# Moving the first FC1 block to just behind head 7, and transposing heads 8 and 9 by DMA between the weight loads, in a fused attention and FFN kernel

## The chip, the cores and the metric

The kernel runs on one core of one Trainium2 chip. The metric is the device time of one execution in microseconds (us), taken on the slowest core, of which there is one here. Several executions are timed and their median is quoted, with the range in brackets. Every run used below was in the fast state, with a granted TensorE clock of 0.998 to 1.0, except where a lower one is named.

PE is the tensor engine (matmuls), ACT the scalar engine, DVE the vector engine, POOL is GpSimd, and SP the engine that issues most DMAs here. "L228" in a profile line is line 228 of that kernel's source.

## The reference, cut to what matters

The attention has B·H = 32 heads of 768 tokens and 64 dimensions. Each q and each k row is assigned to its nearest of 16 centroids, and a query sees only those keys that have its own cluster. The output goes through a feed-forward network with weights 512x2048 and 2048x512.

```python
q_assign = argmax(einsum('bhsd,hcd->bhsc', q_n, c_n))      # k_assign alike
mask     = q_assign[:, :, :, None] == k_assign[:, :, None, :]
scores   = where(mask, scale * q @ k.T, -1e9)
attn     = exp(scores - max) / (sum + 1e-9)
x        = (attn @ v) as (3072 tokens, 512)
h        = x @ w_in                                         # FC1
out      = (gelu(h) @ w_out)                                # FC2, exact gelu
```

## The kernel before

Everything is written by hand into one list of timed events; the "times" only decide the program order of each engine, and each engine then works through its own instructions in that order. For each head, POOL splits q and k (fp32) into a high and a low fp16 half. The 128-token tiles are transposed to `T` (channels on the partitions). PE computes the assignment scores (`asn`), DVE turns them into one-hot rows `oh`, and those are transposed too and written into 16 additional rows of `T`, so that the score matmul adds the mask by itself. ACT exponentiates, PE multiplies by v (the "AV" matmuls), DVE normalises.

There are two ways to transpose. Heads below `PT` use PE with a copy out of PSUM by DVE; the later ones use the DMA transpose, issued from SP:

```python
def tr_pe(i, w, copy=None, pool=None):                      # 6 PE transposes, one copy
    ...
    for j in range(N):
        nc.tensor.transpose(t_ps[:, j*128:(j+1)*128], st[:, w, j, :], ident)
    (copy or nc.vector.tensor_copy)(Ts[i][:, w, :], t_ps)

def tr(i):                                                  # one DMA for q and k
    nc.sync.dma_start_transpose(out=Ts[i]..., in_=st...)

def asn(i, which, halves=True):                             # 6 short matmuls for q or k
    if which == 0:
        asns[i] = ps_a.tile([128, 512], FP32, tag="asn", name="asn_ps")   # ps_a has ONE buffer
    ...
def onehot(i, halves=True): ...                             # three DVE instructions, frees asn_ps
def ohtr(i): ...                                            # one DMA transpose for two heads
def aug(i):                                                 # four DVE copies ohT -> rows 64..79 of T
    ...
PT = 10
FC1 = {(9, 3): 0, (18, 0): 1, (26, 0): 2}                   # FC1 of batch 0 in head 9, slot 3
for n in range(1, 8):
    at(T[n] + 0.5, load_w, n)                               # one weight chunk per head, from POOL
for h in range(4, NH):
    ...                                                     # split, v cast, load of head h + 4
    if h >= PT:
        at(max(T[pair] - {10: 25.0, 12: 25.0, 14: 35.0}.get(pair, 29.0) + ..., sp_t + 3.5), tr, h)
for h in range(PT, NH):
    ...                                                     # asn, onehot, ohtr and aug, ahead of need
```

Each head has six slots: a score matmul pair, a few FC2 matmuls as filler once FC1 has run (`FILL`), AV of the head before. FC1 itself is one dense block of some 21 us per batch.

The softmax here doesn't subtract the row's maximum and nothing guards it: scores larger than these inputs give would overflow.

Of the kernel before, what the change touches and what calls it, by code (L numbers as in the profile page):

```python
# [20 lines left out]
def kernel(  # L21
# [64 lines left out]
    load(1)  # L86
    nc.sync.dma_start(out=v_raw, in_=v[0, 0].rearrange("(p n) d -> p n d", p=128))
    load(2)
    load(3)
# [57 lines left out]
    def tr_pe(i, w, copy=None, pool=None):  # L147
        if i not in Ts:
            Ts[i] = t_pool.tile([128, 2, S], FP16, tag="T", name="T")
        st = sts[i]  # L150
        pl, tag = pool or (ps_o, "op")
        t_ps = pl.tile([128, S], FP16, tag=tag, name="tr_ps")
        for j in range(N):
            nc.tensor.transpose(t_ps[:, j * 128:(j + 1) * 128], st[:, w, j, :], ident)  # L154
        (copy or nc.vector.tensor_copy)(Ts[i][:, w, :], t_ps)  # L155
# [23 lines left out]
    tr_pe(0, 0, copy=nc.scalar.copy, pool=(ps_sc, "sc"))  # L179
    warm(1, 256)  # L180
    nc.vector.tensor_scalar_add(cent_norm, cent_norm, 1e-6)
    nc.vector.reciprocal(cent_rnorm, cent_norm)
    nc.vector.tensor_tensor(cent_hl[:, 0], cent_sb.unsqueeze(1).to_broadcast([H * C, 2, D]),
                            cent_rnorm.unsqueeze(2).to_broadcast([H * C, 2, D]), op=ALU.mult)
# [13 lines left out]
    def tr_halves(i, w):  # L198
        for e, (pl, tag, copy) in enumerate(((ps_sc, "sc", nc.scalar.copy),
                                             (ps_o, "op", nc.vector.tensor_copy))):  # L200
            t_ps = pl.tile([128, S], FP16, tag=tag, name="tr_ps")
            for j in range(N // 2):
                nc.tensor.transpose(t_ps[:, j * 128:(j + 1) * 128],
                                    sts[i][:, w, e * (N // 2) + j, :], ident)
            copy(Ts[i][:, w, e * QB:(e + 1) * QB], t_ps[:, 0:QB])
# [12 lines left out]
    def asn(i, which, halves=True):  # L218
# [6 lines left out]
        for j in range(N):  # L225
# [4 lines left out]
            else:  # L230
                for e in range(2):
                    nc.tensor.matmul(a_ps[:, j, which, 0], t[:, js], c_all[:, e, chs],
                                     start=(e == 0), stop=(e == 1))

# [34 lines left out]
    def one_pe(i):  # L269
        oh = ohs[(i // 2) % NOH]  # L270
        e = i % 2
        t_ps = ps_o.tile([128, S], FP16, tag="op", name="oh_ps")
        for j in range(N):
            nc.tensor.transpose(t_ps[:, j * 128:(j + 1) * 128],
                                oh[:, j].rearrange("p a b c -> p (a b c)"), ident)
        nc.vector.tensor_scalar(Ts[i][D:D + C, 1, :], t_ps[64 * e + 32:64 * e + 32 + C, :],  # L276
                                -1.0, None, op0=ALU.add)
        nc.vector.tensor_scalar(Ts[i][D:D + C, 0, :], t_ps[64 * e:64 * e + C, :],  # L278
                                float(VAL), None, op0=ALU.mult)
# [69 lines left out]
    def fin(i, pe=False):  # L349
        b, h = divmod(i, H)  # L350
        m = h // 2
        if m == 0:
            xts[b] = x_pool.tile([128, NM, S], FP16, tag="xt", name="xt")
        xt, x_tok = xts[b][:, m, :], xtoks.pop(i)
        if pe:
            pl, tag = (ps_a, "asn") if i == 6 else (ps_o, "op")
            t_ps = pl.tile([128, S], FP16, tag=tag, name="fin_ps")
            for j in range(N):
                nc.tensor.transpose(t_ps[:, j * 128:(j + 1) * 128],  # L359
                                    x_tok[:, j].rearrange("p a d -> p (a d)"), ident)  # L360
            nc.vector.tensor_copy(xt, t_ps)
        else:
            nc.sync.dma_start_transpose(
                out=xt.rearrange("c (n p) -> c n p", p=128),
                in_=x_tok.rearrange("p n a d -> p (n a d)"))
# [3 lines left out]
    early = []  # L369

    def fc1_early():
        for t in range(2):
            early.append(ps_o.tile([128, 512], FP32, tag="op", name="hp_early"))
        for m in range(NM - 1):
            for t in range(2):
                nc.tensor.matmul(early[t][:, 0:QB], w_in_sb[:, m, 0:128],
                                 xts[0][:, m, t * QB:(t + 1) * QB],
                                 start=(m == 0), stop=False)
                yield

    def fc1(b, f):
        if f == 0:
            gs[b] = []
        if b == 0 and f == 0:
            g = g_pool.tile([128, S], FP16, tag=f"g{f}", name=f"g{f}")
            for t in range(2):
                ts = slice(t * QB, (t + 1) * QB)
                nc.tensor.matmul(early[t][:, 0:QB], w_in_sb[:, NM - 1, 0:128],
                                 xts[0][:, NM - 1, ts], start=False, stop=True)
            gs[b].append(g)  # L390
        else:
            hp = ps_sc.tile([128, 2, 512], FP32, tag="sc", name="hp")
            for m in range(NM):
                for t in range(2):
                    nc.tensor.matmul(hp[:, t, 0:QB],  # L395
                                     w_in_sb[:, m, f * 128:(f + 1) * 128],
                                     xts[b][:, m, t * QB:(t + 1) * QB],
                                     start=(m == 0), stop=(m == NM - 1))
            g = g_pool.tile([128, S], FP16, tag=f"g{f}", name=f"g{f}")
            nc.scalar.activation(g.rearrange("p (t q) -> p t q", t=2),  # L400
                                 hp[:, :, 0:QB], ACT_FN.Gelu, bias=0.0, scale=1.0)
            gs[b].append(g)
            if b == 0 and f == 1:
                for t in range(2):
                    nc.scalar.activation(gs[0][0][:, t * QB:(t + 1) * QB], early[t][:, 0:QB],
                                         ACT_FN.Gelu, bias=0.0, scale=1.0)
# [22 lines left out]

    def load_w(n):  # L430
        nc.gpsimd.dma_start(out=w_chunks[n][0], in_=w_chunks[n][1])


    warm(1)
    cent_tr()
    tr_halves(0, 1)
    nc.scalar.copy(sts[1][:, 1, :, 0:D], k1_raw)
    nc.gpsimd.tensor_sub(sts[1][:, 1, :, D:2 * D], k1_raw, sts[1][:, 1, :, 0:D])
    warm(1)
    asn(0, 0, halves=False)  # L440
    asn(0, 1, halves=False)
    onehot(0, halves=False)
# [25 lines left out]
    def slot(i, c):  # L468
# [5 lines left out]
        if i >= 10:  # L474
# [5 lines left out]
    def start_early():  # L480
        filler[0] = fc1_early()

    def start_fc2(b):
# [3 lines left out]
    PT = 10  # L487
    FC1 = {(9, 3): 0, (18, 0): 1, (26, 0): 2}
# [3 lines left out]
        (0, 0): ((1, 'trk'),),  # L492
        (0, 1): ((1, 'asq'),),
        (0, 2): ((1, 'ask'), (1, 'oneh'),),
        (0, 3): ((2, 'trq'),),
        (0, 4): ((1, 'onep'),),
        (0, 5): ((2, 'trk'), (2, 'asq'),),
        (1, 0): ((3, 'trq'),),
        (1, 1): ((2, 'ask'), (2, 'oneh'), (3, 'trk'),),
        (1, 2): ((0, 'av0'), (0, 'av1'),),  # L500
        (1, 3): ((0, 'av2'), (2, 'onep'),),
        (1, 4): ((3, 'asq'), (3, 'ask'), (0, 'av3'), (3, 'oneh'),),
        (1, 5): ((0, 'av4'), (0, 'av5'), (0, 'norm'),),
        (2, 0): ((4, 'trq'),),
        (2, 1): ((3, 'onep'),),
        (2, 2): ((1, 'av0'), (1, 'av1'),),
        (2, 3): ((4, 'trk'), (4, 'asq'),),
        (2, 4): ((1, 'av2'), (1, 'av3'), (4, 'ask'),),
        (2, 5): ((1, 'av4'), (1, 'av5'),),
        (3, 0): ((4, 'oneh'), (1, 'norm'), (5, 'trq'),),  # L510
        (3, 1): ((4, 'onep'),),
        (3, 2): ((2, 'av0'), (2, 'av1'), (2, 'av2'),),
        (3, 3): ((5, 'trk'), (5, 'asq'),),
        (3, 4): ((0, 'fin'), (2, 'av3'), (5, 'ask'),),
        (3, 5): ((2, 'av4'), (2, 'av5'),),
        (4, 0): ((5, 'oneh'), (2, 'norm'), (6, 'trq'),),
        (4, 1): ((5, 'onep'),),
        (4, 2): ((3, 'av0'), (3, 'av1'),),
        (4, 3): ((6, 'trk'), (6, 'asq'),),
        (4, 4): ((3, 'av2'), (3, 'av3'), (6, 'ask'),),  # L520
        (4, 5): ((3, 'av4'), (3, 'av5'),),
        (5, 0): ((6, 'oneh'), (3, 'norm'), (7, 'trq'),),
        (5, 1): ((6, 'onep'),),
        (5, 2): ((4, 'av0'), (4, 'av1'), (7, 'asq'),),
        (5, 3): ((7, 'trk'), (4, 'av2'),),
        (5, 4): ((2, 'fin'), (7, 'ask'),),
        (5, 5): ((4, 'av3'), (4, 'av4'), (4, 'av5'),),
        (6, 0): ((7, 'oneh'), (4, 'norm'), (8, 'trq'),),
        (6, 1): ((7, 'onep'),),
        (6, 2): ((5, 'av0'), (5, 'av1'),),  # L530
        (6, 3): ((8, 'trk'), (5, 'av2'),),
        (6, 4): ((5, 'av3'), (8, 'asq'), (8, 'ask'),),
        (6, 5): ((8, 'oneh'), (5, 'av4'), (5, 'av5'), (5, 'norm'),),
        (7, 0): ((9, 'trq'),),
        (7, 1): ((8, 'onep'),),
        (7, 2): ((6, 'av0'), (6, 'av1'),),
        (7, 3): ((9, 'trk'), (9, 'asq'),),
        (7, 4): ((6, 'av2'), (6, 'av3'), (9, 'ask'),),
        (7, 5): ((6, 'av4'), (9, 'oneh'), (6, 'av5'),),
        (8, 0): ((6, 'norm'), (4, 'fin'),),  # L540
        (8, 1): ((9, 'onep'),),
        (8, 2): ((7, 'av0'), (7, 'av1'),),
        (8, 3): ((7, 'av2'),),
        (8, 4): ((7, 'av3'), (7, 'av4'),),
        (8, 5): ((7, 'av5'),),
        (9, 0): ((7, 'norm'),),
        (9, 1): ((6, 'fin'),),
        (9, 2): ((8, 'av0'),),
        (9, 3): ((8, 'av1'),),
        (9, 4): ((8, 'av2'), (8, 'av3'),),  # L550
        (9, 5): ((8, 'av4'), (8, 'av5'),),
        (10, 0): ((8, 'norm'),),
# [7 lines left out]
    for i in range(NH + 1):  # L560
        for c in range(N):
            if (i, c) in FC1:
                b = FC1[i, c]
                at(t, fill, 1000)
                for f in range(NF):
                    at(t + f * 1.3, fc1, b, f)
# [103 lines left out]
```

## Time and profile before

The time before is 302.01 us (301.86 to 302.23, three runs). The profiled execution has a span of 300.2 us. The busy line of its page gives, for each engine, the busy time, its share of the span and the number of instructions:

```profile
PE 295.1 (98%) x3098; PEld 185.6 (62%) x3098; DVE 125.2 (42%) x286; ACT 214.0 (71%) x273; POOL 108.1 (36%) x183
```

PE is the limit, but 98% doesn't say by how much: pipelined matmuls cover short waits with their modelled ends. The Trainium skill ("Trainium Kernel Development and Optimization", section "Performance Expectations") calls matmul busy time a bad metric, because matmuls are pipelined, of how close a kernel is to what the chip can do.

So I use another account throughout. For each matmul record I take the distance from its start to the next one's start, and subtract what that kind of matmul takes when nothing delays it: 55.5 ns for a 128-column transpose, 162.5 for 384 columns, 215.7 for 512, 109 for 256, 30 for an AV matmul, 25 for an assignment. What remains is stall. The Trainium skill ("TensorE: Matmul & The Clock Gate", section "Wait — 56ns, not 53.3ns?") gives N/2.4 GHz plus about 2.5 ns, that is 55.6 and 215.7 ns; the trace agrees with 55 to 56 and, for most matmuls of 512 columns, 215 to 216 ns (nearly all others 218 to 219). For the kernel before (the text on record has 288.0 and 8.3 for the sums, since it counted one warm-up matmul of 256 columns like one of 512; the tables here have that put right):

| stretch (us from the span's start) | stall, us |
|---|---|
| 0 to 4.4, warm-up, with 427 ns for most 512-column matmuls | 1.92 |
| 4.4 to 9.43, prologue up to the first scores | 1.78 |
| 9.43 to 54.25, attention alone, 9.5 heads | 3.69 |
| all the rest | 1.01 |
| sum of stalls; sum of PE work | 8.40; 287.9 |

In the attention-only stretch three other engines are nearly full. This is the line of the windows view (stretch, its length, busy time and instructions of PE, PEld, DVE, ACT and POOL, granted clock, DMA share, GB/s):

```profile
9.43:54.25 44.82, 43.84 (x709) 33.99 (x710) 37.89 (x84) 41.99 (x57) 42.93 (x66) 1.00 1.16 268
```

The timeline view (start, duration, engine, source line, operation, output<-inputs, count, idle time before it and its releaser) has the arrival of the centroids, the first scores, the start of the FC1 block, and the slow DMA transposes that run beside the w_out loads.

```profile
3.23 0.26 ACT L170 ACTIVATE cent_sq<-cent_sb 128x64 f32<-128x64 f32 x1 [0.56 <-DMA cent_sb<-in_centroids_dram]
...
9.43 0.50 PE L320 MATMUL sc_ps<-T 80*128 80x384 f16 x2
...
54.76 5.53 PE L395 MATMUL hp<-xt,w_in_sb 128*128 128x384 f16 x33
...
45.09 8.63 SPq L210 DMA_TRANSPOSE T<-st  x2
```

The last line (SPq is SP's queue of DMA instructions) is two q/k transposes whose two issues stretch over 8.63 us of the SP queue; in the trace records they took 9.3 and 9.7 us from issue to landing, where the median of this kernel's q/k transposes is 4.7.

### The profile page before, as it was taken

The numbers are of one execution on the slowest core, as the hardware profiler recorded it, in microseconds if no ns is written. First come the engines' busy times: TensorE is split into PE (matmuls) and PEld (weight loads), VectorE is DVE, ScalarE is ACT, GpSimd is POOL, SyncE is SP. The second block draws the span as 40 slices with busy tenths as digits, with TensorE's granted clock in tenths as the row PEclk, the third lists the DMA queues.
The fourth block names the chain that finished last, engine by engine and source line by source line (L and its number), as shares of the span: only waits on it lengthen the run. The fifth ranks groups of instructions, "written<-read, shape, count | busy, mean of one in ns | idle before, by whom it ended". The sixth has DMA issues, their size and how long they took to land.

```text
span 300.2 us, 7392 instructions
## 1 busy us (share of the span) xinstructions
PE 295.1 (98%) x3098; PEld 185.6 (62%) x3098; DVE 125.2 (42%) x286; ACT 214.0 (71%) x273; POOL 108.1 (36%) x183
## 2 busy tenths in 40 slices
PE   8899999999999999999999999999999999999996
PEld 4677777666666666666566666666566565555444
DVE  5898897102664732132365732122353413000112
ACT  5699999965888888856788888865788883466000
POOL 4999999999034004574444004600000000000000
PEclk9999999999999999999999999999999999999999
DMA  6999999994279258979489237866032221000122
GB/s 210 352 305 259 264 264 209 228 239 114 54 204 208 63 120 214 201 177 193 99 215 200 63 90 211 169 89 131 2 87 63 64 58 40 36 2 0 44 97 70
DMA packets 74065, 42.85 MB, mean 143 GB/s; under 512 B 54320, under 2 KB 71088, under 8 KB 74032
## 3 DMA queue, kind: packets, MB, share of 16 engines
q1 hardware_dynamic: 69520, 38.09, 52.4%
q0 software_dynamic: 4224, 4.19, 8.4%
q8 instruction: 24, 0.39, 0.5%
q10 hardware_dynamic: 288, 0.10, 0.1%
q14 instruction: 9, 0.07, 0.1%
HBM read 27.30 MB, written 6.29 MB: 112 GB/s over the span
## 4 chain that ended last, share of the span: by engine, by line
PE 89%; DVE 6%; ACT 3%; DMA 1%; issue 0%
PE hp L395 27%; PE op L421 25%; PE sc_ps L320 18%; PE x_ps L335 10%; PE op_alt L421 3%; ACT p_sb L323 3%; PE asn_ps L228 3%; PE tr_ps L154 1%; DVE T L155 1%; DMA q_raw<-in_q_dram 1%; DVE T L276 1%; DVE T L278 1%; DVE x_tok L346 1%; PE fin_ps L359 1%; DVE asum L241 1%; DVE oh L249 0%
## 5 line engine op out<-in xcount | busy, mean ns | idle before, releaser
L323 ACT ACTIVATE p_sb<-sc_ps 128x768 f16<-128x768 f32 x192 | 148.7, 811 | 21.3 <-PE sc_ps L320 13.0
L421 PE MATMUL op<-w_out_sb,g 128*128 128x512 f16 (+1 forms) x352 | 97.1, 371 | 0.0
L320 PE MATMUL sc_ps<-T 80*128 80x384 f16 x384 | 93.7, 324 | 0.6 <-ACT p_sb L323 0.4
L395 PE MATMUL hp<-xt,w_in_sb 128*128 128x384 f16 x504 | 85.0, 326 | 0.0
L400 ACT ACTIVATE g<-hp 128x768 f16<-128x768 f32 x63 | 51.1, 811 | 37.2 <-PE hp L395 37.1
L335 PEld LDWEIGHTS <-p_sb 128*128 128x128 f16 x1152 | 53.7, 97 | 29.8 <-DVE x_tok L346 0.6
L395 PEld LDWEIGHTS <-w_in_sb 128*128 128x128 f16 x504 | 47.9, 98 | 30.4
L335 PE MATMUL x_ps<-vaug,p_sb 128*128 128x65 f16 x1152 | 58.5, 193 | 0.0
L421 PEld LDWEIGHTS <-g 128*128 128x128 f16 x416 | 38.9, 97 | 30.2
L132 POOL CAST st<-q_raw 128x384 f16<-128x384 f32 x30 | 15.6, 520 | 77.3 <-DMA q_raw<-in_q_dram 56.0
L425 DVE COPY o_sb<-op 128x512 f32<-128x512 f32 (+1 forms) x22 | 14.8, 672 | 55.0 <-PE op L421 54.9
L241 DVE TENSOR_REDUCE asum<-asn_ps 128x192 f32<-128x384 f32 x30 | 16.7, 557 | 50.4 <-PE asn_ps L228 50.3
L320 PEld LDWEIGHTS <-T 80*128 80x128 f16 x384 | 26.5, 97 | 4.7 <-DVE T L278 0.5
L135 POOL TENSOR_TENSOR st<-k_raw,st 128x384 f16<-128x384 f32 x30 | 27.4, 913 | 2.4
L133 POOL TENSOR_TENSOR st<-q_raw,st 128x384 f16<-128x384 f32 x30 | 27.4, 912 | 2.5
L345 DVE RECIPROCAL rec<-x_ps 128x6 f32<-128x6 f32 x32 | 6.2, 193 | 42.4 <-PE x_ps L335 42.4
L228 PEld LDWEIGHTS <-T 128*128 128x128 f16 x360 | 15.6, 96 | 5.5 <-DVE T L155 0.8
L228 PE MATMUL asn_ps<-c_all,T 128*128 128x32 f16 x360 | 18.0, 177 | 0.4 <-DVE T L155 0.2
L346 DVE TENSOR_TENSOR x_tok<-x_ps,rec 128x384 f16<-128x384 f32 x32 | 17.8, 558 | 1.1
L143 POOL CAST vaug<-v_raw 128x384 f16<-128x384 f32 x32 | 16.1, 508 | 0.0
L134 POOL CAST st<-k_raw 128x384 f16<-128x384 f32 x30 | 15.3, 510 | 0.0
L284 DVE TENSOR_SCALAR T<-ohT 16x768 f16<-16x768 f16 x22 | 9.4, 428 | 6.9 <-DMA ohT<-oh 6.4
(73 smaller groups left out, 144.6 us busy)
## 6 DMA issues: line engine op xcount, KB each, us to landing
q_raw<-in_q_dram SPq DMA_DIRECT2D x32, 192.0 KB, 4.0
k_raw<-in_k_dram SPq DMA_DIRECT2D x32, 192.0 KB, 4.1
v_raw<-in_v_dram SPq DMA_DIRECT2D x32, 192.0 KB, 4.2
out_dram<-o_sb SPq DMA_DIRECT2D x23, 256.0 KB, 2.3
w_in_sb<-in_moe_w_in_dram POOLq DMA_DIRECT2D x4, 512.0 KB, 9.8
w_out_sb<-in_moe_w_out_dram POOLq DMA_DIRECT2D x4, 512.0 KB, 10.4
T<-st SPq DMA_TRANSPOSE x22, 4.7
ohT<-oh SPq DMA_TRANSPOSE x11, 2.8
```

What stands on the lines that cost most here:

```text
L133: nc.gpsimd.tensor_sub(st[:, 0, :, D:2 * D], q_raw, st[:, 0, :, 0:D])
L135: keng.tensor_sub(st[:, 1, :, D:2 * D], k_raw, st[:, 1, :, 0:D])
L143: nc.gpsimd.tensor_copy(va[:, :, 0:D], vraws.pop(i))
L228: nc.tensor.matmul(a_ps[:, j, which], t[:, js], c_all[:, :, chs], start=True, stop=True)
L241: nc.vector.tensor_reduce(out=asum, in_=a_ps.rearrange("p n w l c -> p n w c l"), axis=AX.X, op=ALU.add)
L320: nc.tensor.matmul(s_ps[:, t, 0:QB], Ts[i][0:D + C, 1, c * 128:(c + 1) * 128], Ts[i][0:D + C, 0, t * QB:(t + 1) * QB], start=True, stop=True)
L323: nc.scalar.activation(ps[i][:, c, :].rearrange("p (t q) -> p t q", t=2), s_ps[:, :, 0:QB], ACT_FN.Exp, bias=0.0, scale=float(scale))
L335: nc.tensor.matmul(x_ps[:, j], ps[i][:, ch, j * 128:(j + 1) * 128], va[:, ch, 0:D + 1], start=(ch == 0), stop=(ch == N - 1))
L346: nc.vector.tensor_tensor(xtoks[i - i % 2][:, :, i % 2, :], x_ps[:, :, 0:D], rec.to_broadcast([128, N, D]), op=ALU.mult)
L395: nc.tensor.matmul(hp[:, t, 0:QB], w_in_sb[:, m, f * 128:(f + 1) * 128], xts[b][:, m, t * QB:(t + 1) * QB], start=(m == 0), stop=(m == NM ...
L400: nc.scalar.activation(g.rearrange("p (t q) -> p t q", t=2), hp[:, :, 0:QB], ACT_FN.Gelu, bias=0.0, scale=1.0)
L421: nc.tensor.matmul(op[:, 0:w], gs[b][f][:, js], w_out_sb[:, f, ms], start=(f == 0), stop=(f == NF - 1))
```

## The change

The intent is to take PE work away and to shorten the stretch in which attention runs with no filler. Heads 8 and 9 go over to the DMA transpose (`PT = 8`). Transposes beside w_out loads are slow, so they are put between the weight loads: w_in is loaded earlier, and w_out is held back by a one-element copy of head 9's transposed k, which makes POOL wait for the transpose. FC1 of batch 0 then starts right behind head 7. The q, k and v loads are reordered by first use, and the prologue is recast in smaller pieces. The core of the diff:

```diff
-    load(1)
-    nc.sync.dma_start(out=v_raw, ...)
-    load(2)
-    load(3)
+    for i, w in ((1,'q'), (1,'k'), (2,'q'), (2,'k'), (0,'v'), (3,'q'), (3,'k'), (1,'v'), (2,'v'), (3,'v')):
+        nc.sync.dma_start(out=raws[i]["qkv".index(w)], ...)
-    tr_pe(0, 0, copy=nc.scalar.copy, pool=(ps_sc, "sc"))
-    warm(1, 256)
-    nc.vector.tensor_tensor(cent_hl[:, 0], cent_sb..., cent_rnorm..., op=ALU.mult)
+    nc.scalar.activation(cent_hl[:, 0, 0, :], cent_sb, ACT_FN.Copy, bias=0.0, scale=cent_rnorm)
+    nc.scalar.copy(cent_hl[:, 0, 1, :], cent_hl[:, 0, 0, :])
     ... (a second warm-up matmul goes; q of head 0 is transposed in two halves,
     ...  its one-hot is made before k's)
+    def hold(h):
+        nc.gpsimd.tensor_copy(half[0:1, 0:1], Ts[h][0:1, 1, S - 1:S])
-    PT = 10
-    FC1 = {(9, 3): 0, (18, 0): 1, (26, 0): 2}
+    PT = 8
+    FC1 = {(8, 0): 0, (18, 0): 1, (26, 0): 2}
     ... (the plan of pieces for heads 0 to 7 is laid out anew; transpose and copy are apart)
-    for n in range(1, 8):
-        at(T[n] + 0.5, load_w, n)
+    for n, tw in enumerate((-1, 0, 2)):
+        at(tw, load_w, n + 1)                       # w_in
+    LOADS = {8: (), 9: (), 10: (12,), 11: (13,), 12: (14, 15), 13: (16, 17), 14: (18,)}
+        if h == 9:
+            at(sp_t + 0.04, hold, 9)
+            for n in range(4, 8):
+                at(sp_t + 0.041, load_w, n)         # w_out
+        if h in (8, 9):
+            at(sp_t + 0.026, tr, h)
-        ta, to, tg = (17.5, 12.0, 5.0) if pair >= 12 else (12.5, 7.0, 3.0)
+        ta, to, tg = (20.5, 15, 5) if pair == 8 else (17.5, 12, 5) if pair == 10 else (17.5, 12.0, 5.0)
```

At the seam, head 7's remaining AV work and pieces of FC1 are interleaved (`fc1_first`), so that FC1 does not wait for head 7's normalisation.

## The prediction

> **What bounds the kernel now.** The tensor engine. The busy table gives PE 295.1 us of 300.2; the waits show only 1.6 us of PE waits. Overlap hides small bubbles, so I compared start-to-start spacings of the matmul records with their usual value: 55-56 ns for a 128-column transpose, 162 for 384 columns, 216 for 512, 30 for the 65-column AV, 25 for the 32-column assignment. The Trainium skill ("TensorE: Matmul & The Clock Gate", section "Wait — 56ns, not 53.3ns?") gives N/2.4 GHz plus 2.5 ns; 55.6 and 215.7 ns agree with this trace. The sum over all matmuls is 288.0 us; 8.3 us are stalls: 1.9 in the slow warm-up before 4.4 us, 1.7 from 4.4 to 9.4 us (prologue), 3.7 in the attention-only stretch 9.4-54.9 us (9.5 heads), 1.0 in all the rest. In 9.4-54.9 the windows view has ACT 42.7, DVE 38.0, POOL 43.6 of 45.5 us: three engines nearly full, about 4.8 us per head.
>
> **What the change does.**
> 1. Heads 8, 9 are transposed by DMA: 24 q/k transposes, 12 one-hot transposes and two warm matmuls leave PE: 36 x 55.5 ns = 2.0 us plus 0.43 us. Nearly all of this counts.
> 2. FC1 starts after 8 heads instead of 9.5: PE work is only moved, so this gains just the stalls of the shorter stretch. I estimate 34.9 us of PE work against 8 heads x 4.7-4.85 us = 37.6-38.8: stall 2.7-3.9, formerly 3.7. With the rearranged pieces I take 3.2: gain 0.5.
> 3. Prologue: half-size copies on ACT and DVE, cent_hl's 0.83 us multiply off DVE, q's assignment before k's. One-hot done about 0.4 us earlier, first scores near 9.0 instead of 9.43; 0.43 us of that is the warm matmuls already counted, so 0-0.2 more.
> 4. DMA: two T transposes and one ohT transpose more; w_in moves up (last chunk issued near 21 us instead of 27.3), w_out waits for head 9's transpose.
>
> **Timing of the new dependences (estimates).** POOL takes 2.85 us per split, 0.5 per v cast, 0.78 per weight issue. Splits of heads 8 and 9 end near 34.5 and 38; the first transposes of before took up to 9.7 us to land, so head 9 is there by 43-46, before its assignment near 52. The hold stalls POOL about 5 us; four w_out issues end near 48; each took 9.4-12.8 us to land, all by about 62, FC2 starts near 68. POOL then resumes with head 10, whose T is needed near 65: the tightest place. The skill ("DMA: Bandwidth & Descriptors", "Issuing engines are not separate DMA queues") says all queues share 16 DMA engines; here the DMA share is above 1 from 10 to 70 us, so lateness there is the main risk.
>
> **Sum.** 302.0 - 2.4 - 0.5 - 0.1 = 299.0 us; 8 in 10: 297.4 to 300.8. Faster by over 2% (under 296) needs nearly all prologue and attention stalls gone: 0.04; within 2%: 0.94; slower: 0.02.
>
> **What would show each step.** Groups: 38 fewer PE matmuls. Timeline: first scores at 8.9-9.1 us; the first long FC1 run near 47 us (54.8 before), FC2 near 68. Stalls before FC1 near 7 us in total, unchanged to 1 us lower; PE waits after FC1 near zero. Windows: ACT and DVE still over 80% in the attention stretch. DMA view: transposes of heads 8, 9 landing before 46 us; w_out by 62. POOL timeline: a gap of 3-8 us at the hold.
>
> **What would make it wrong.** T of head 10 or 11 late: PE, in program order, then stops at their assignment (1-4 us slower). The shorter stretch being more bound by DVE or ACT than I think: gain shrinks to about 2 us. The rearranged pieces removing most bubbles: 297.5.

## More of the kernel before

One more place of the timeline is needed later. It shows SP, DVE and PE near 100 us, where the pair of heads 14 and 15 hands over to head 16:

```profile
92.64 1.39 SPq L210 DMA_TRANSPOSE T<-st  x1
94.13 1.81 SPq L265 DMA_TRANSPOSE ohT<-oh  x1
...
97.46 0.54 DVE L284 TENSOR_SCALAR T<-ohT 16x768 f16<-16x768 f16 x1
...
98.12 0.30 PE L228 MATMUL asn_ps<-c_all,T 128*128 128x32 f16 x6
...
100.72 0.35 DVE L249 TENSOR_TENSOR oh<-asum,asn_ps 128x192 f16<-128x192 f32 x1
...
102.16 0.31 PE L228 MATMUL asn_ps<-c_all,T 128*128 128x32 f16 x6
```

The first two lines are the DMA transpose of the one-hot of heads 14 and 15 and, in front of it in SP's queue, a q/k transpose. The next is the first copy of that transposed one-hot, then come the first assignment of head 16, the end of head 16's one-hot, and the first assignment of head 17. PE didn't wait here: the assignment tile was free 1.09 us (102.16 − 100.72 − 0.35) before PE came to it.

## The result, and the profile after

The changed kernel took 300.29 us (300.18 to 301.43, four runs) against 301.95 us (301.86 to 302.23, four runs) for the kernel before in the same rounds. The ratio is 0.995 (0.9932 to 0.9968), so it is within 2%. Here and below a ratio is the mean time of one kernel's fast runs over that of the other's of the same rounds, so it is not quite the ratio of the medians quoted. The page's busy line and the windows line of the attention-only stretch, after:

```profile
PE 292.0 (98%) x3060; PEld 182.1 (61%) x3060; DVE 124.5 (42%) x284; ACT 212.6 (71%) x275; POOL 109.1 (37%) x184
```

```profile
9.39:46.30 36.91, 36.26 (x589) 27.21 (x590) 30.22 (x67) 34.95 (x48) 33.22 (x52) 1.00 1.03 241
```

There are 38 fewer PE instructions, as predicted. The stretch now covers 8 heads in 36.91 us, 4.61 per head against 4.72 (44.82/9.5), still with ACT at 95% and DVE at 82%. The timeline after, first the marks of before, then SP and POOL at the hold, ACT at the start of FC1, then PE and ACT where head 8 follows FC1:

```profile
3.55 0.26 ACT L183 ACTIVATE cent_sq<-cent_sb 128x64 f32<-128x64 f32 x1 [0.89 <-DMA cent_sb<-in_centroids_dram]
...
9.39 0.82 PE L369 MATMUL sc_ps<-T 80*128 80x384 f16 x4
...
46.30 1.26 PE L459 MATMUL x_ps<-vaug,p_sb 128*128 128x65 f16 x36
47.39 1.14 PE L437 MATMUL hp<-xt,w_in_sb 128*128 128x384 f16 x6
...
34.33 4.75 SPq L228 DMA_TRANSPOSE T<-st  x2
...
41.98 0.43 SPq L74 DMA_DIRECT2D v_raw<-in_v_dram  x1
55.77 1.37 SPq L301 DMA_TRANSPOSE ohT<-oh  x1
57.25 3.34 SPq L228 DMA_TRANSPOSE T<-st  x2
...
41.37 0.18 POOL L526 CAST half<-T 1x1 f32<-1x1 f16 x1 [2.39 <-DMA T<-st]
41.49 3.01 POOL L529 DMA_DIRECT2D w_out_sb<-in_moe_w_out_dram  x4
...
47.04 1.28 ACT L449 ACT_TABLE_LOAD   x1
50.43 0.81 ACT L449 ACTIVATE g<-hp 128x768 f16<-128x768 f32 x1 [2.10 <-PE hp L437]
...
68.97 0.48 PE L369 MATMUL sc_ps<-T 80*128 80x384 f16 x2
69.29 1.46 PE L516 MATMUL op<-w_out_sb,g 128*128 128x512 f16 x6
...
72.70 0.48 PE L369 MATMUL sc_ps<-T 80*128 80x384 f16 x2
73.02 0.38 PE L516 MATMUL op<-w_out_sb,g 128*128 128x512 f16 x1
73.53 0.48 PE L369 MATMUL sc_ps<-T 80*128 80x384 f16 x2
...
69.84 1.28 ACT L372 ACT_TABLE_LOAD   x1
71.13 6.77 ACT L372 ACTIVATE p_sb<-sc_ps 128x768 f16<-128x768 f32 x9
```

The first scores start at 9.39 us, hardly before the 9.43 of the kernel before, though the centroids too arrived 0.32 us later in this execution. The FC1 block is reached at 47.39 us (predicted near 47). The transposes of heads 8 and 9 landed at 38.88 and 41.31 us in the trace records, and POOL's gap at the hold was 2.39 us. In the last lines head 8's slots hold a score pair and one FC2 matmul, 0.54 us of PE work (2 x 0.1625 + 0.2157), while each exponential takes ACT 0.75 us (6.77/9): PE starts the next pair at 73.53, 0.29 us after it could. No AV work stands beside it, since head 7's was done before FC1.

The account of stalls on PE, before, after, and for a second copy of the changed kernel (first experiment), in us:

| | before | after | after, again |
|---|---|---|---|
| PE work | 287.9 | 285.6 | 285.6 |
| warm-up (to 4.4) | 1.92 | 1.89 | 1.90 |
| prologue | 1.78 | 2.10 | 1.72 |
| attention stretch | 3.69 | 2.71 | 2.71 |
| FC1 block of batch 0 | 0.01 | 0.38 | 0.38 |
| seam to heads 8 and 9, then up to 124 us | 0.29 | 0.76 | 1.73 |
| from 124 us to the last matmul | 0.71 | 0.72 | 0.72 |
| last matmul to the end | 3.04 | 3.38 | 3.36 |

From before to after the profiled spans differ by 1.8 us: PE work −2.32, prologue +0.32, attention stretch −0.98, FC1 block and seam about +0.8, last matmul to the end +0.3, the rest near zero. The 0.3 us at the end aren't chance: all twelve profiles with the q/k transposes of heads 8 and 9 on the DMA have them, and the two without (before and pe_in_fc1) don't. The last DMA isn't the reason, since it landed 1.55 us after its issue before and 1.56 after; the time lies behind that landing, and no run isolates its cause.

The second copy had 0.97 us more stall between the seam and 124 us. The reason is visible in its timeline at the handover from the pair 14/15 to heads 16 and 17:

```profile
91.80 2.91 SPq L228 DMA_TRANSPOSE T<-st  x1
94.80 1.56 SPq L301 DMA_TRANSPOSE ohT<-oh  x1
...
97.09 0.30 PE L246 MATMUL asn_ps<-c_all,T 128*128 128x32 f16 x6
...
101.89 0.30 PE L246 MATMUL asn_ps<-c_all,T 128*128 128x32 f16 x6 [0.83 <-DVE oh L285]
...
98.18 0.35 DVE L333 TENSOR_SCALAR T<-ohT 16x768 f16<-16x768 f16 x1 [1.43 <-DMA ohT<-oh]
98.55 0.97 DVE L336 TENSOR_SCALAR T<-ohT 16x768 f16<-16x768 f16 x1
99.54 0.56 DVE L333 TENSOR_SCALAR T<-ohT 16x768 f16<-16x768 f16 x1
100.11 0.35 DVE L336 TENSOR_SCALAR T<-ohT 16x768 f16<-16x768 f16 x1
100.49 0.56 DVE L277 TENSOR_REDUCE asum<-asn_ps 128x192 f32<-128x384 f32 x1
...
101.48 0.35 DVE L285 TENSOR_TENSOR oh<-asum,asn_ps 128x192 f16<-128x192 f32 x1
```

PE computed head 16's assignment at 97.09, about 1 us earlier than in the kernel before. DVE sat 1.43 us in front of the copy from `ohT`, a DMA transpose that landed at 98.16, and head 16's one-hot comes after the four copies in program order. So the tile was free only at 101.83, and PE waited in front of head 17's assignment. Compared with before (assignment of head 16 at 98.12, landing at 97.44), PE came 1.03 us earlier and the landing 0.72 us later: both ate the slack. The landing was later because the issue was: head 15's one-hot was ready at 92.84 (93.49 before), but the q/k transpose in front of the one-hot transpose held SP until 94.71 (94.03 before). In all fourteen profiles the one-hot transpose was issued 0.1 us after the issue of the q/k transpose in front of it ended.

### The profile page after: what moved, and what is told of

It reads as the page before. It is cut to its first block, busy times and chain, and to the rows that moved or that the text cites. A ratio compares the mean times of both kernels' runs of the same rounds, so it can differ in the third digit from the quotient of the medians.

```text
span 298.3 us, 7315 instructions
## 1 busy us (share of the span) xinstructions
PE 292.0 (98%) x3060; PEld 182.1 (61%) x3060; DVE 124.5 (42%) x284; ACT 212.6 (71%) x275; POOL 109.1 (37%) x184
## 4 chain that ended last, share of the span: by engine, by line
PE 92%; ACT 3%; DVE 2%; issue 1%; POOL 1%; POOLq 0%; ACTq 0%
PE op L516 24%; PE hp L494 21%; PE sc_ps L369 20%; PE x_ps L384 11%; PE hp L437 7%; PE op_alt L516 3%; PE asn_ps L246 3%; ACT p_sb L372 2%; PE tr_ps L160 1%; PE oh_ps L311 1%; PE fin_ps L416 1%; ACT g L449 0%; ACT L372 0%; DVE T L327 0%; DVE T L317 0%
## 5 line engine op out<-in xcount | busy, mean ns | idle before, releaser
L372 ACT ACTIVATE p_sb<-sc_ps 128x768 f16<-128x768 f32 x192 | 147.2, 810 | 18.9 <-PE sc_ps L369 11.4
L516 PE MATMUL op<-w_out_sb,g 128*128 128x512 f16 (+1 forms) x352 | 98.6, 371 | 0.0
L384 PEld LDWEIGHTS <-p_sb 128*128 128x128 f16 x1116 | 51.9, 97 | 28.9 <-DVE x_tok L395 0.9
L384 PE MATMUL x_ps<-vaug,p_sb 128*128 128x65 f16 x1116 | 57.0, 193 | 0.0
```

The costliest lines, as they stand in the source:

```text
L372: nc.scalar.activation(ps[i][:, c, :].rearrange("p (t q) -> p t q", t=2), s_ps[:, :, 0:QB], ACT_FN.Exp, bias=0.0, scale=float(scale))
L384: nc.tensor.matmul(x_ps[:, j], ps[i][:, ch, j * 128:(j + 1) * 128], va[:, ch, 0:D + 1], start=(ch == 0), stop=(ch == N - 1))
L516: nc.tensor.matmul(op[:, 0:w], gs[b][f][:, js], w_out_sb[:, f, ms], start=(f == 0), stop=(f == NF - 1))
```

## The experiments

Twelve runs were made, ten of new kernels and two of the changed kernel again, all with a correct result. They were to tell apart these theories. The first (A) says that the gain is the PE work taken away, so that each us of transposes put back costs one us. A rival (C) says that the stretch ahead of FC1 is paced by ACT and DVE, so that PE work removed there is partly handed back as waiting. A third (D), formed after the first runs, says that the order of the SP queue makes the one-hot transposes late and gives the gain back after FC1; D2 is a variant of it. The words beside a letter in a quoted text say which claim is meant.

| run | median us (range) | ratio to before (95%) | stall 78 to 106 us | stall in all |
|---|---|---|---|---|
| changed kernel, first | 300.29 (300.18–301.43) | 0.9950 (0.9932–0.9968) | 0.24 | 8.56 |
| after_again | 301.25 (300.70–301.91) | 0.9973 (0.9962–0.9984) | 1.19 | 9.16 |
| pe_in_fc1 | 301.99 (301.57–302.10) | 0.9994 (0.9983–1.0006) | 0.21 | 8.81 |
| dma_late | 312.78 (312.34–313.90) | 1.0349 (1.0336–1.0362) | – | – |
| nohold | 301.68 (301.04–302.66) | 0.9988 (0.9972–1.0003) | 2.53 | 10.90 |
| dma_qk_late | 306.09 (304.22–308.28) | 1.0137 (1.0106–1.0168) | 4.44 | 13.21 |
| late_aug | 301.73 (301.52–302.02) | 0.9988 (0.9976–1.0000) | 1.70 | 10.13 |
| fill8 | 301.50 (301.23–301.87) | 0.9981 (0.9969–0.9994) | 1.87 | 9.50 |
| cent_pow | 301.20 (300.53–301.38) | 0.9965 (0.9953–0.9977) | 0.96 | 9.55 |
| after_third | 300.75 (300.12–301.22) | 0.9952 (0.9940–0.9964) | 1.31 | 9.44 |
| sp_early | 303.14 (302.20–304.63) | 1.0034 (1.0014–1.0054) | – | 12.97 |
| sp_early_fill8 | 302.65 (302.26–303.40) | 1.0018 (1.0005–1.0031) | – | 11.69 |
| oh8_pe2 | 300.68 (300.38–302.50) | 0.9966 (0.9946–0.9986) | 0.65 | 8.24 |

The stalls are of the one profiled execution of each kernel, the times of all. The kernel before had medians of 302.05, 302.06, 302.20 and 302.14 us in the four batches. The batch of dma_qk_late, late_aug, fill8 and cent_pow, and that of oh8_pe2, had no control, so these can be compared with the changed kernel only through the ratios.

### after_again and after_third: the changed kernel as it is

No edit. These are the controls.

> The changed kernel, unaltered, as the control of this call and for a second profile. Theory A (the gain is the 2.0 us of PE work that heads 8 and 9 no longer need, plus about 0.9 us of stalls saved in the shorter attention stretch, of which about 0.85 us come back in and after the first FC1 block): 1.5 to 2.0 us below the kernel before, the same stalls in the same places. If the 0.3 us later arrival of the centroids and the 0.3 us longer tail were only variation of that one profile, they go away here and the profiled span is 0.3 to 0.6 us shorter.

> The changed kernel again, as the control of this call. Theory D, formed from the runs so far: the changed kernel leaves the SP queue standing from 42.4 to 55.8 us in front of the transposed one-hot codes of heads 8 and 9, and the transposes and loads held up behind it crowd the DMA at 60 to 98 us; how late the next one-hot transposes land differs from execution to execution, and PE stalls 0 to 1.7 us for it. Then: 300.2 to 301.9 us, wider than the 0.5 us of before, and in the profile a stall at about 80 or 102 us of 0 to 1.1 us.

The same kernel gave ratios of 0.9950, 0.9973 and 0.9952 in three batches, and single runs from 300.12 to 301.91 us, whereas the kernel before stayed within about half a us in each batch. So a difference of 0.5 us between two variants of the changed kernel, taken in different batches, says little. Both controls have the wait of head 17's assignment: 0.99 and 0.63 us.

### pe_in_fc1: heads 8 and 9 transposed by PE, inside FC1

```diff
-            at(sp_t + 0.04, hold, 9)
-        if h in (8, 9):
-            at(sp_t + 0.026, tr, h)
-        elif h >= PT:
+        if h >= 10:
+    for n, (h, which) in enumerate(((8, 0), (8, 1), (9, 0), (9, 1))):
+        at(T[8] - 16.8 + 1.3 * n, tr_pe, h, which)
+    ... (asn, onehot, and PE transposes of the one-hot, during FC1)
```

> FC1 still starts after head 7, but heads 8 and 9 are transposed on PE inside the FC1 block (24 q/k and 12 one-hot transposes come back; hold removed since there is nothing to hold for). Theory A: 36 x 55.5 ns = 2.0 us slower than the changed kernel, so equal to the kernel before within 0.5 us. Rival B (the gain comes from starting FC1 early, the transposes hid in waits): within 0.5 us of the changed kernel.

PE work was 287.6 us, 2.0 more than in the changed kernel, exactly the 36 transposes, and of the change only the place of FC1, the order of the loads and the prologue were left. The kernel is 0.7 us slower than the control of the same batch (301.99 against 301.25) and the same as before within its interval. The largest reason why the 0.7 is less than 2.0 is that the PE version lost no time to late one-hot transposes: stall from 78 to 106 us was 0.21 us against 1.19 in the control. So the removed PE work counts, and about 1 us of it was handed back through the DMA path in that control. (The one-hot transpose of heads 14 and 15 didn't land earlier in the PE version, but at 99.34 us against 98.16; PE itself came to head 16's assignment 2.64 us later, and so after the landing.) Against the profile of the first run of the changed kernel, where the transposes happened to land in time, the spans differ by nearly the whole 2.0 us (300.3 and 298.3); there 0.3 us more stall in the PE version and 0.3 us less at its end cancel.

### dma_late: the kernel before, with the DMA transposes alone

`PT = 8`, the hold and the new order of the loads go into the kernel before; FC1 stays in head 9.

```diff
-    PT = 10
+    PT = 8
     FC1 = {(9, 3): 0, (18, 0): 1, (26, 0): 2}
+        if pair == 8:
+            ta, to, tg = 8.0, 4.2, 0.9
```

> The kernel before with only the DMA transposes of heads 8 and 9 (and the loads, hold and orders that they need); FC1 still starts in head 9, the prologue and the plan are the old ones. Theory A in its strict form (every us of PE work counts wherever it is taken away): 1.5 to 2.0 us faster than before. Rival C (the attention stretch is paced by ScalarE's exponentials and VectorE, so PE work taken out of it only becomes PE stall, and starting FC1 early is what turns it into time): under 0.7 us faster, and the stalls before FC1 grow from 7.3 to over 8.5 us.

The time rose to 312.78 us. The waits view (what waited, for what: total, times, longest) names it:

```profile
PE sc_ps L320 <- DVE T L287: 9.0, 1, 9.0
```

Head 8's scores waited 9.0 us for the copies of its one-hot, whose DMA transpose was issued at 45.50, beside the w_out loads, and landed at 56.00. This run had a granted clock of 0.978, so its excess over the kernel before isn't only that wait. It shows why the DMA transposes and the new place of FC1 go together in this plan: FC1's 21 us between heads 7 and 8 give the one-hot transpose of heads 8 and 9 the time to land. Other ways to give it that time weren't tried here.

### dma_qk_late: only the q/k transposes by DMA, one-hot by PE, FC1 in its old place

```diff
-        (6, 0): ((7, 'oneh'), (4, 'norm'), (8, 'trq'),),
+        (6, 0): ((7, 'oneh'), (4, 'norm'), ),
     ... (the same for trk of 8 and trq, trk of 9; hold and loads as in the changed kernel)
```

> A cleaner try at the transposes alone: the kernel before, with only the 24 q/k transposes of heads 8 and 9 moved to DMA (with the load order and the hold); their one-hot codes stay on PE at the old places, FC1 still starts in head 9. 24 x 55.5 ns = 1.33 us of PE work leaves the attention stretch. Theory A strict (PE work counts wherever it is removed): 1.0 to 1.4 us faster than before, stalls before FC1 unchanged at about 7.3 us. Rival C (the stretch is paced by ScalarE and VectorE): at most 0.5 us faster, stalls before FC1 up by 0.8 us or more.

This takes 24 transposes, 1.33 us of PE work, out of the stretch before FC1. FC1 started at 53.93 us, 0.83 earlier than the 54.76 of before, of which 0.13 were gained ahead of the first scores (9.30 instead of 9.43), and the stall of that stretch rose from 3.69 to 4.31. So some 0.7 of 1.3 us arrived; the rest became stall in a stretch in which ACT, DVE and POOL are nearly full. The total got worse for another reason, again in the waits view (some of this kernel's runs had a granted clock down to 0.987):

```profile
PE sc_ps L320 <- DVE T L287: 3.3, 1, 3.3
```

That is head 10's scores, at 82.46 us, waiting for the transposed one-hot of heads 10 and 11. Both theories about the stretch thus hold in part, and lateness of DMA transposes after FC1 is the larger cost.

### nohold: the changed kernel without the hold

```diff
-            at(sp_t + 0.04, hold, 9)
```

> The changed kernel without the copy that holds w_out; the four w_out loads are then issued about 2.4 us earlier, while the transposes of heads 8 and 9 are in flight. Theory A: the transposes land later, up to 46 us, still before their assignment at 49.8 and 52.6 us, so the same time within 0.3 us. Rival (the hold is needed): assignment of head 8 or 9 waits for DMA, 1 us or more slower than the changed kernel.

It took 301.68 against the control's 301.25 us. The transposes of heads 8 and 9 themselves landed in 3.7 to 4.4 us, just as with the hold, so this run doesn't show the hold doing what it is meant for. What grew is the wait of the assignments:

```profile
PE asn_ps L246 <- DVE oh L285: 2.0, 2, 1.5
```

The one-hot transpose of heads 14 and 15 landed at 99.90 us here, against 97.57 to 98.42 in the three profiles of the changed kernel. The kernel differs from pe_in_fc1 only in how heads 8 and 9 are transposed (neither holds w_out), and its stall from 78 to 124 us is 2.66 against 0.34 us. Both issue w_out at the same point of the program. But the landing was only 0.56 us earlier in pe_in_fc1 (99.34), whereas PE came to head 16's assignment 1.62 us later (99.73 against 98.11). So PE's earlier arrival explains more of the wait than a slower DMA path, and that the additional DMA transposes delay the later ones isn't shown. It is one execution of each.

### late_aug: the DVE copies from ohT behind head n+2's one-hot

```diff
-            at(T[pair] - tg, aug, pair)
+            at(T[pair] - (tg if pair == 8 else 3.28), aug, pair)
```

> The changed kernel with one reordering: in VectorE's program the copies of a pair's transposed one-hot codes come after the next pair's first one-hot instead of before it. The profiles of the control and of the kernel without hold show PE stopping 0.99 and 1.70 us at 102 to 104 us, in front of an assignment whose PSUM buffer is free only after a one-hot that stands in VectorE's queue behind a copy waiting for a DMA transpose. If that is why the changed kernel measured 300.2 once and 301.3 in the control, this stall is zero here, and the time is 300.0 to 300.5 with runs closer together. If the spread has another cause, it measures like the control, 300.7 to 301.9.

The wait of the assignments is gone from the list, which confirms that DVE's program order caused it. But other waits took its place: 0.37 us at 80.85 for the copies into `T`, which now come too late for the scores, and at 83.33 this one, on the normalisation that DVE reaches later:

```profile
PE x_ps L384 <- DVE x_tok L395: 0.9, 1, 0.9
```

The median was 301.73 us, a ratio of 0.9988, no better than the controls' 0.9973 and 0.9952. DVE's queue is one line: whatever waits in it delays the rest. The Trainium skill ("TensorE: Matmul & The Clock Gate", section "Architectural detail: the array is 16× 32×32, not 1× 128×128") says that the queues of ACT and DVE are strictly first in, first out. For DVE the profiles of after_again (1.43 us in front of the first copy, with the one-hot behind it) and of this run agree.

### fill8: more FC2 matmuls in head 8

```diff
+    for c in range(2, N):
+        spare += 2 - FILL[8, c]
+        FILL[8, c] = 2
+    ... (as many fewer in heads 9 to 11)
```

> The changed kernel with four more FC2 matmuls in the slots of head 8, taken from heads 9 to 11. Head 8 has no AV work of head 7 beside it, since that was done before FC1; its slots hold two score matmuls and one FC2 matmul (0.54 us) against one exponential of 0.72 us, and PE waits for ScalarE by 0.29 and 0.1 us. If so, the 0.4 us of stalls at 73 to 75 us go and no others come: 0.3 to 0.5 us faster than the changed kernel. If the stall only moves to heads 9 to 11, no difference.

The stall of head 8's slots fell from 0.43 to 0.12 us, so the seam was understood. The gain didn't reach the end: the assignments of heads 13 and 17 waited, by 0.63 and 1.04 us of stall.

```profile
PE asn_ps L246 <- DVE oh L285: 1.3, 2, 0.9
```

### cent_pow: a shorter centroid chain in the prologue

```diff
-    nc.gpsimd.memset(half, 0.5)
+    nc.gpsimd.memset(half, -0.5)
-    nc.gpsimd.tensor_tensor(cent_norm, cent_ssq, half, op=ALU.pow)
+    nc.gpsimd.tensor_tensor(cent_rnorm, cent_ssq, half, op=ALU.pow)
-    nc.vector.tensor_scalar_add(cent_norm, cent_norm, 1e-6)
-    nc.vector.reciprocal(cent_rnorm, cent_norm)
```

> The changed kernel with a shorter centroid chain in the prologue: the power on GpSimd gives the reciprocal norm itself (exponent -0.5), which drops an addition and a reciprocal of VectorE, 0.34 us and two hand-overs. In six profiles so far the first scores come 5.83 to 5.85 us after the centroids are in (new prologue) or 6.1 to 6.2 (old one). If the centroid chain is what bounds the prologue, the first scores come about 5.45 us after the centroids, 0.3 to 0.4 us earlier, and the kernel is faster by that. If the q and k chains bound it, nothing changes.

Two DVE instructions leave the chain from the centroids to the first scores. From the centroids' arrival to the first scores it took 6.44 us (3.20 to 9.64), more than the 5.83 to 6.08 of most runs with the new prologue. This execution can't test the idea, though. Its critical view, followed back from the first scores, runs through head 0's k, which landed at 3.91 us, and not through the centroids; so it does in nohold (k at 4.27 us, 6.41 us from centroids to scores). In the first profile of the changed kernel the chain did run through the two DVE instructions (4.80 to 5.16 us). Which load ends last thus changes between executions, and whether the shorter chain helps where the centroids bind stays open.

### sp_early and sp_early_fill8: SP's later work put into its idle time

In the changed kernel SP has nothing to issue from 42.4 to 55.77 us, as the timeline above shows: the one-hot transpose of heads 8 and 9 stands at the head of its queue and waits for the one-hot. Here the transposes of heads 10 and 11 and four heads' loads are issued in front of it.

```diff
-    LOADS = {8: (), 9: (), 10: (12,), 11: (13,), 12: (14, 15), 13: (16, 17), 14: (18,)}
+    LOADS = {8: (), 9: (), 10: (12, 13, 14, 15), 11: (), 12: (16,), 13: (17,), 14: (18,)}
-            at(max(T[pair] - {14: 35.0, 10: 27.0, 12: 27}.get(...)..., tr, h)
+            at(max(T[pair] - {14: 35.0, 10: 40.0, 12: 32.0, 16: 36.0}.get(...)..., tr, h)
```

The second kernel has fill8's edit as well.

> The changed kernel with another order in the SP queue only: the q/k transposes of heads 10 and 11 and the loads of heads 14 and 15 come before the one-hot transpose of heads 8 and 9, those of heads 12, 13, 16 and 17 are moved up as well. Theory D: the SP queue no longer stands idle at 42 to 55 us, no PE stall over 0.2 us at 78 to 106 us, 300.0 to 300.6 us with less spread, 0.5 to 1.0 us faster than the control. Rival E (the DMA engines themselves have too much to do there, the order does not matter): the stalls stay or move, the time is within 0.3 us of the control. Risk: w_out lands later (58 us in the changed kernel) and FC2, from 69 us, waits.

> The same with the four FC2 matmuls moved to head 8. Theory D with the seam at head 8: another 0.3 to 0.4 us, 299.7 to 300.3 us, about 0.7% faster than before.

Both are slower than before, by 0.3 and 0.2%, at 303.14 and 302.65 us. The timeline of SP in sp_early shows why:

```profile
47.70 16.66 SPq L228 DMA_TRANSPOSE T<-st  x2
64.46 1.23 SPq L301 DMA_TRANSPOSE ohT<-oh  x1
```

The two transposes now meet the w_out loads. Their issue held SP for 16.66 us (3.34 for the same two in the changed kernel), so the one-hot of heads 8 and 9 is transposed at 64.46 instead of 55.77, and everything behind it is later:

```profile
PE asn_ps L246 <- DVE oh L285: 3.0, 3, 1.3
```

Of the 4.4 us by which this profiled span exceeds the changed kernel's, 1.0 lies in the prologue (first scores at 10.42), 1.5 at the end of FC1 and 1.9 between 78 and 124 us. Filling SP's idle time with these transposes is worse, so theory D gave a wrong remedy; whether the gap itself costs anything, these runs don't show.

### oh8_pe2: the one-hot of heads 8 and 9 by PE

No hold, fill8's edit, and PE transposes for the one-hot of heads 8 and 9, so that nothing on SP waits for them.

```diff
-            at(T[pair] - to, ohtr, pair)
-            at(T[pair] - tg, aug, pair)
+            if pair == 8:
+                for n in (8, 9):
+                    ... at(T[8] - 10.3 + 3.9 * (n % 2) + 0.01 * z, piece, n)   # one_mm, one_k, one_q
```

> q/k transposes of heads 8 and 9 by DMA as in the changed kernel, but their one-hot codes transposed on PE in the FC1 block (12 x 55.5 ns = 0.67 us of PE work comes back), no hold, and the four FC2 matmuls moved to head 8. It differs from the kernel without hold only in the one-hot of heads 8 and 9 and the FC2 slots. The order test has shown that transposes beside w_out are slow (17 us to landing), so its fix falls; the narrower theory D2 is left: what delays the later one-hot transposes is the SP queue waiting from 43 to 56 us for the one-hot of heads 8 and 9. If D2 holds, the loads after head 11's transpose start near 54.7 us (60.6 in the changed kernel), as in the kernel that transposes heads 8 and 9 on PE, PE has no stall over 0.2 us at 78 to 106 us, and the time is 299.8 to 300.4 us with a spread under 0.7 us. If the extra DMA traffic as such is the cause, a stall of 0.5 us or more stays there, and the time is 300.8 or more.

The median is 300.68 us, and the stalls of the profiled execution are the fewest of all (8.24 us), against 0.7 us more PE work. The loads on SP that were to start near 54.7 us started at 59.4, so the mechanism that I had expected wasn't what happened: the q/k transposes of heads 10 and 11, now first in SP's queue, took 15.8 and 10.3 us beside w_out. The wait of head 17's assignment was still there, with 0.45 us. It is within the spread of the changed kernel, so I claim no improvement. No version that ran beats the changed kernel clearly.

### What the runs show together about the late one-hot

For nine of the fourteen profiled executions: the start of head 16's assignment on PE, the landing of the one-hot transpose of heads 14/15, the start of head 17's assignment, and the stall just before it (trace records, us). 

| run | asn 16 | landing | asn 17 | stall |
|---|---|---|---|---|
| before | 98.12 | 97.44 | 102.16 | 0 |
| changed kernel | 97.45 | 97.57 | 101.30 | 0 |
| after_again | 97.09 | 98.16 | 101.89 | 0.99 |
| after_third | 97.72 | 98.42 | 102.17 | 0.63 |
| cent_pow | 97.71 | 98.55 | 102.29 | 0.76 |
| fill8 | 97.38 | 98.47 | 102.24 | 1.04 |
| oh8_pe2 | 97.39 | 98.19 | 101.65 | 0.45 |
| nohold | 98.11 | 99.90 | 103.64 | 1.70 |
| pe_in_fc1 | 99.73 | 99.34 | 103.54 | 0 |

Where there is a stall, head 17's assignment starts 3.73 to 3.77 us after the landing (3.46 in oh8_pe2), which is the length of DVE's copies plus the one-hot; and the stall is roughly the landing minus the start of head 16's assignment, less 0.1 us (less 0.35 in oh8_pe2). The two sp_early kernels, not in the table, have the same wait with a shorter chain: 2.9 us from landing to assignment, stalls of 0.49 and 0.54. In the kernel before the landing came 0.7 us ahead of head 16's assignment. That slack was used up from both sides: in the table's variants of the changed kernel that stall, PE came 0 to 1.0 us earlier and the landing 0.7 to 2.5 us later. The landing moves because SP is free later: head 15's one-hot was ready 0.5 to 2.6 us before its transpose was issued, and each time the q/k transpose in front of it, whose issue took 1.4 to 3.4 us, stood in the way. Why that issue takes longer in one execution than in another, the runs don't settle.

## Why the prediction was right or wrong

The predicted time was 299.0 us with a range of 297.4 to 300.8. Measured were 300.29 us in the first batch, inside the range and within 2%, as was held most likely; in the two later batches the changed kernel's medians were 301.25, outside the range, and 300.75. The centre was too low by 1.3 us, and these are the terms of the sum:

- **"36 x 55.5 ns = 2.0 us plus 0.43 us. Nearly all of this counts."** The 2.0 us of transposes is right in size: PE work fell by 2.32 us in all, and pe_in_fc1, which puts them back, has 2.0 us more work. The 0.43 us of the two warm matmuls was wrong as a gain. It is 0.32 us in fact, since one of them has 256 columns, and they only filled waiting time: the prologue's stall rose by as much (1.78 to 2.10) and the first scores came at 9.39 instead of 9.43.
- **Prologue, "first scores near 9.0 ... 0-0.2 more".** The centroids arrived between 3.0 and 3.7 us in different executions. From arrival to first scores it took 5.83 to 5.96 us in seven profiles with the new prologue, against 6.09 to 6.20 in three with the old one, but 6.08, 6.41 and 6.78 in three more with the new one. So it is better by about 0.3 us where the centroids come last, and not always. In the profiled execution the later arrival took that away; in after_again the first scores were at 9.02. The term for the prologue and the warm matmuls together was thus 0.53 predicted, 0.0 to 0.4 measured.
- **Shorter stretch, "I take 3.2: gain 0.5".** The mechanism was right and the size too small: the stretch's stall is 2.71 us, and the gain 0.98. That equals the lower end of the range I had worked out (2.7 to 3.9). The pace became 4.61 us per head instead of 4.72; how much of this the rearranged pieces brought, no run isolates.
- **"PE waits after FC1 near zero."** This is the step that failed. "PE work is only moved" left out that moving the FC1 block makes a new seam: 0.37 us in the FC1 block (most of it one wait of 0.26 us up to 51.29: the third FC1 tile in the scores' PSUM pool, which has two buffers, needs the one that ACT's first Gelu read until 51.24; ACT's table load had ended at 48.3, and the Gelu itself had waited 2.10 us for PE) and about 0.43 in head 8, whose first slots have 0.54 us of PE work for exponentials of 0.75 us. fill8 removed the latter (0.12 left). On top comes the wait of head 17's assignment, 0 to 1.7 us by execution, which gives part or most of the freed PE time back: pe_in_fc1, with 2 us more PE work and no such wait, lost only 0.7 us to the control.
- **The risk "T of head 10 or 11 late".** The right kind, in the wrong place. In the changed kernel the transposes of heads 10 and 11 landed at 61.0 and 62.8 us, in time. Late was the one-hot transpose of heads 14 and 15, some 35 us further on, and it reached PE through DVE's program order and the single assignment tile. dma_qk_late did show a wait for heads 10 and 11 (3.3 us), when FC1 stayed in its old place.
- **Timing of the dependences.** Heads 8 and 9 landed by 41.31 us (said: before 46), w_out by 58.4 (by 62), FC2 started at 69.29 (near 68). POOL's gap of 2.39 us was just below the stated 3 to 8.

In sum: −3.0 predicted; +0.5 for prologue and warm matmuls, −0.5 for the stretch, +0.8 for FC1 and the seam, +0.3 at the end, which gives the −1.8 us of the profiled spans but for rounding. That the first batch came within 1.3 us of the centre is in part luck: a gain that was too small by half offset a seam that was left out, and its profiled execution had no late one-hot, as later ones had. In the other batches up to about 1 us more goes to the wait of head 17's assignment.

## What to carry to other kernels

When a change takes work off the bounding engine, look downstream for every hand-over that had just been in time before: the engine now arrives earlier there, and a DMA that doesn't move with it, or comes later because its queue is held by the one in front, eats the gain. Such a lateness can reach the bounding engine by a detour, here a copy on an in-order vector engine and a PSUM tile with one buffer, so list the slack of those hand-overs (0.7 us here) before predicting that waits stay at zero. And work that is moved isn't neutral: check what stands beside its old and new neighbours, and count filler instructions such as warm-up matmuls as a gain only if nothing waits behind them.

## What the Trainium skill lacked or had wrong

- "DMA: Bandwidth & Descriptors", section "Issuing engines are not separate DMA queues", says that all issuers share the same 16 DMA engines, and that a sequencer's time for starting a DMA is usually small relative to the DMA itself. The first agrees: w_out, issued from POOL, slowed transposes issued from SP. For the DMA transposes here that time isn't small: a one-hot transpose kept SP for 1.2 us of 2.75 us to its landing, and in sp_early one q/k transpose beside w_out kept SP for 8.97 of 17.45 us.
- The same page, section "Rules for kernel authors", says that "A transpose next to ordinary DMAs needs nothing". That is about correct data, and all results here were correct. It lacks the cost in time: in the three profiles of the changed kernel 3.7 to 7.0 us from issue to landing of a q/k transpose (median 4.4 to 4.5), but 7.7 to 17.5 us, in the seven profiles that have such, for one issued after w_out's loads and over 3 us before the last of them landed.
- No page that I found says how much the landing of one and the same DMA transpose varies between executions of one kernel: 97.57, 98.16 and 98.42 us from the span's start here in three profiles, which at a hand-over with 0.7 us of slack decides between no stall and 1 us.
